# Sliding-window attention and a routed expert layer in one kernel: queries in one transfer, and the expert blocks begun in attention's last steps

## The chip, the cores and the metric

The kernel runs on one core of one Trainium2 chip. The metric is the device time of one execution in microseconds (us). Before the change three runs gave 413.17, 415.88 and 416.45 us; their median is 415.88. PE is TensorE (PEld its weight loads), DVE is VectorE, ACT is ScalarE, POOL is GpSimd, SP is SyncE, which here only issues transfers.

## The reference

```
# attention: B=8 batches, H=8 heads, S=576 positions, D=64
scores = (q @ k.T) / sqrt(D) - slope[h] * |i - j|,  kept where 0 <= i - j < 128
x = softmax(scores) @ v                        # as 4608 tokens x 512

# layer on x: w1_dense, w2_dense, and E=8 experts of 512 x 512 twice
y_dense = relu(x @ w1_dense) @ w2_dense
e = argmax(x @ w_gate);  g = softmax(x @ w_gate)[e]
out = y_dense + g * (relu(x @ w1[e]) @ w2[e])
```

Inputs and outputs are float32.

## The kernel before

**Attention.** A unit `u` is four heads of one batch: 16 units, two to a batch. A unit has three steps (query tiles 0-1, 2-3, and the tail 4), so there are `NS` = 48 steps. In step `n` the program emits, in this order: `flip` of step n-3 (PE transposes the normalized output, ACT copies it twice, L531), `scores` of step n (mask L405 and q times k L417 on PE, exp on ACT L428), `norm` of step n-2 (DVE L496, L497; POOL copies the rows, L503), parts of routing, `attend` of step n-1 (PE L481), parts of the dense layer (`dense1` L689/L696, `dense2` L704/L712), the preparation of the next unit, and `lo` of step n (DVE L447, the low halves of the weights). PE, ACT and DVE run this order as written (`manual_schedule`); POOL's order is set by the framework.

**Queries and keys.** A unit's `kraw` and `qraw` have one buffer each. k comes in one transfer: 18 rows of the sequence to a partition, 4608 contiguous bytes. q comes in five transfers (L140): 4 rows to a partition four times, then 2 rows. In step 0 of a unit DVE transposes the next unit's k (`turn`, L162), in step 1 its q; ACT rounds k in step 1 (L172) and q in step 2 (L169). The rounding of k puts the positions back in order by a strided write; q stays permuted within a tile, and the mask and the token numbers are built to that order. v comes in five transfers (L154) of 256-byte rows into three buffers. All loads after the first are issued on SP's queue, in program order.

**Routing and experts.** After a batch's two units its gate is computed (`gate_a` to `gate_d`), its 576 rows are scattered to their experts' regions in HBM (`xs_dram`, POOL L643), and its dense outputs to `ys_dram` (POOL L713). Then `NB` = 43 blocks of 128 rows follow: `fetch` (SP L901 loads a block's rows xr and yr), `turn_x` (PE L916, DVE L922), `layer1` (PE L937, ACT L945), `turn_h` (PE L952, ACT L956), `layer2` (PE L964, DVE L972, and POOL L973 scatters to the output). The first `NE` = 16 blocks hold rows of the first six batches, and their table (`route_early`) is computed while the last units run. The other 27 need all batches, the late table, and eight pairs of fill transfers (`late_fill`, SP L878 and L882) that pad the experts' last blocks. Blocks begin at loop step n = 50, two steps after the last `attend`; the dense work of batches 6 and 7 lies between the first blocks.

## Time and profile before

| | us |
|---|---|
| profiled execution | 411.29 |
| its span | 409.6 |
| median of three runs | 415.88 |
| PE / DVE / ACT / POOL busy | 339.0 / 269.8 / 261.6 / 192.9 |

The span is what the trace covers; 1.7 us of the profiled execution lie around it. Attention fills about the first 274 us, the blocks the rest up to 400 us. Busy shares are means over these two parts, so the rows below are taken from stretches.

### The profile page before, as it was taken

What the parts mean: (1) busy time and instruction counts of PE and PEld (TensorE: products, weight loads), DVE (VectorE), ACT (ScalarE), POOL (GpSimd) and SP (SyncE); (2) the same over time, 40 slices, a digit from 0 to 9 for tenths busy, and PEclk for the clock granted to TensorE, in tenths of its full rate; (3) what the DMA queues carried; (4) which work ended last, traced back from release to release, by engine and by line L of the source; (5) the groups of instructions that cost most, each with busy time, mean ns of one, the idle gap of its engine ahead of it and who ended that gap; (6) DMA issues with size and microseconds to landing.
All of it is one profiled execution on the core that took longest, in us unless ns stands there. A gap on an engine that the chain in (4) does not pass through costs nothing.

```text
span 409.6 us, 12253 instructions
## 1 busy us (share of the span) xinstructions
PE 339.0 (83%) x4659; PEld 215.2 (53%) x4659; DVE 269.8 (66%) x525; ACT 261.6 (64%) x431; POOL 192.9 (47%) x245
## 2 busy tenths in 40 slices
PE   3458887979869998968997996978799799999990
PEld 0245666646555665645664764654455455555540
DVE  6668889787867986957897889752346344444440
ACT  6448847857856986984797786644356445555550
POOL 4012331654765447564566576353457434434431
PEclk9999959989978999997999998999999999999996
DMA  4565678859798779788696965429959999888730
GB/s 146 144 159 142 148 172 193 195 173 238 165 235 180 202 204 218 212 188 225 197 226 195 235 179 116 99 70 338 310 172 323 303 311 324 244 264 234 250 117 1
DMA packets 84986, 82.40 MB, mean 201 GB/s; under 512 B 43583, under 2 KB 71615, under 8 KB 84928
## 3 DMA queue, kind: packets, MB, share of 16 engines
q1 hardware_dynamic: 66852, 48.17, 41.2%
q0 software_dynamic: 17680, 33.12, 31.3%
q8 instruction: 38, 0.62, 0.6%
q10 hardware_dynamic: 396, 0.33, 0.3%
q14 instruction: 20, 0.16, 0.1%
HBM read 64.20 MB, written 28.66 MB: 227 GB/s over the span
## 4 chain that ended last, share of the span: by engine, by line
PE 30%; DMA 19%; DVE 18%; issue 13%; POOL 9%; SPq 6%; ACT 2%; POOLq 1%; ACTq 0%; DVEq 0%
DMA qraw<-in_q_dram 16%; POOL out_dram L973 6%; DVE plo L447 6%; PE yp L704 6%; PE ax L481 6%; SPq L140 5%; DVE qs L162 4%; PE hpm L937 3%; PE y L964 3%; PE hp L689 3%; DVE xf L497 2%; PE lg L566 2%; DMA xr<-xs_dram 2%; DMA xs_dram<-xrow,slot 2%; PE sq L417 1%
## 5 line engine op out<-in xcount | busy, mean ns | idle before, releaser
L481 PE MATMUL ax<-vf,p 128*128 128x65 bf16 (+1 forms) x576 | 66.6, 205 | 28.8 <-DVE xf L497 26.4
L447 DVE TENSOR_TENSOR plo<-p 128x1024 bf16<-128x1024 f32 (+1 forms) x96 | 85.2, 928 | 8.0 <-ACT p L428 7.9
L481 PEld LDWEIGHTS <-p 128*128 128x128 bf16 (+1 forms) x1152 | 62.9, 107 | 41.3 <-DVE xf L497 34.9
L428 ACT ACTIVATE p<-sq 128x1024 f32<-128x1024 f32 (+1 forms) x96 | 69.8, 784 | 4.8 <-PE sq L417 4.6
L973 POOL DMA_INDIRECT out_dram<-yo,xr x43 | 42.4, 986 | 64.5 <-DVE yo L972 54.1
L503 POOL CAST xrow<-xf 128x512 bf16<-128x512 f32 (+1 forms) x48 | 33.2, 700 | 71.5 <-DVE xf L497 66.7
L481 PE MATMUL ax<-vf,plo 128*128 128x65 bf16 (+1 forms) x576 | 66.1, 202 | 0.5 <-DVE plo L447 0.5
L481 PE MATMUL ax<-vl,p 128*128 128x64 bf16 (+1 forms) x576 | 66.2, 201 | 0.0
L481 PEld LDWEIGHTS <-plo 128*128 128x128 bf16 (+1 forms) x576 | 58.7, 106 | 0.7 <-DVE plo L447 0.7
L713 POOL DMA_INDIRECT ys_dram<-yt,slot x40 | 45.7, 1142 | 26.7 <-ACT yt L712 17.9
L643 POOL DMA_INDIRECT xs_dram<-xrow,slot x40 | 46.2, 1154 | 14.6 <-issue 10.2
L922 DVE COPY xTm<-xps 128x512 bf16<-128x512 bf16 x43 | 18.3, 424 | 50.1 <-PE xps L916 46.9
L696 ACT ACTIVATE hTd<-hp 128x256 bf16<-128x256 f32 (+1 forms) x64 | 26.4, 419 | 35.5 <-PE hp L689 34.6
L937 PE MATMUL hpm<-w_all,xTm 128*128 x172 | 44.0, 377 | 5.1 <-DVE yo L972 2.1
L704 PE MATMUL yp<-w_all,hTd 128*128 128x512 bf16 (+1 forms) x160 | 40.6, 381 | 6.7 <-DVE ltsb L559 5.0
L964 PE MATMUL y<-w_all,hTm 128*128 x172 | 44.1, 379 | 0.8 <-ACT hTm L956 0.8
L945 ACT ACTIVATE hr<-hpm,xr 128x512 bf16<-128x512 f32 x43 | 29.6, 687 | 22.5 <-PE hpm L937 19.3
L972 DVE TENSOR_TENSOR yo<-y,yr 128x512 f32<-128x512 f32 x43 | 29.7, 691 | 20.7 <-PE y L964 20.1
L689 PE MATMUL hp<-xTb,w_all 128*128 128x256 bf16 (+1 forms) x256 | 42.4, 296 | 0.6 <-ACT xTb L531 0.3
L956 ACT COPY hTm<-hps 128x512 bf16<-128x512 bf16 x43 | 25.2, 585 | 23.2 <-PE hps L952 23.2
L531 ACT COPY xT<-tp 128x512 f32<-128x512 f32 (+1 forms) x48 | 23.9, 498 | 23.3 <-PE tp L524 23.2
L417 PE MATMUL sq<-qT,kT 32*128 32x256 f32 (+2 forms) x640 | 32.0, 310 | 7.0 <-ACT qT L169 7.0
(146 smaller groups left out, 559.7 us busy)
## 6 DMA issues: line engine op xcount, KB each, us to landing
yr<-ys_dram SPq DMA_DIRECT2D x43, 256.0 KB
kraw<-in_k_dram SPq DMA_DIRECT2D x16, 576.0 KB
vf<-in_v_dram SPq DMA_DIRECT2D x64, 128.0 KB
w_all<-in_moe_w_dram POOLq DMA_DIRECT2D x16, 512.0 KB
qraw<-in_q_dram SPq DMA_DIRECT2D x62, 128.0 KB
xr<-xs_dram SPq DMA_DIRECT2D x43, 130.0 KB
ys_dram<-fill_x SPq DMA_DIRECT2D x8, 256.0 KB
xs_dram<-fill_x SPq DMA_DIRECT2D x8, 130.0 KB
```

What stands on the lines that cost most here:

```text
L417: nc.tensor.matmul(out=sq[g // 2][:, g % 2, i * wid : i * wid + nq], lhsT=kT[32 * g : 32 * g + 32, c, kj * P : kj * P + P], rhs=qT[32 * g ...
L428: nc.scalar.activation(out=p32[:, :, 0:tot], in_=sq[i][:, :, 0:tot], func=ACT.Exp, scale=SCALE,)
L447: nc.vector.tensor_tensor(out=plo[:, :, 0:tot], in0=p32[:, :, 0:tot], in1=phi[:, :, 0:tot], op=ALU.subtract,)
L481: nc.tensor.matmul(out=ax[:rows, i, o0 : o0 + w], lhsT=lhs, rhs=rhs, start=(n == 1), stop=(n == 3 * len(kl)),)
L503: nc.gpsimd.tensor_copy(out=xrow[:rows, qis[0] : qis[0] + nt, hq * 256 : hq * 256 + 256], in_=xf[:rows, 0:nt],)
L643: ins = nc.gpsimd.indirect_dma_start(out=xs_dram[:, :], out_offset=bass.IndirectOffsetOnAxis(ap=slot[:rows, t : t + 1], axis=0), in_=xrow. ...
L689: nc.tensor.matmul(out=hp[:, 0:HF], lhsT=w_all[:, E, 0, kc, c * P : c * P + P], rhs=xTb[:, kc, c0:c1], start=(kc == 0), stop=(kc == 3),)
L704: nc.tensor.matmul(out=yp[:rows, :], lhsT=hT[:, c, t0 * P : t0 * P + rows], rhs=w_all[:, E, 1, c, :], start=(c == 0), stop=(c == 3),)
L713: ins = nc.gpsimd.indirect_dma_start(out=ys_dram[:, :], out_offset=bass.IndirectOffsetOnAxis(ap=slots[b][:rows, t : t + 1], axis=0), in_=y ...
L937: nc.tensor.matmul(out=hp, lhsT=xT[:, kc, :], rhs=w_all[:, bass.DynSlice(er, 1), 0, kc, :], start=(kc == 0), stop=(kc == 3),)
L964: nc.tensor.matmul(out=y, lhsT=hT[:, c, :], rhs=w_all[:, bass.DynSlice(er, 1), 1, c, :], start=(c == 0), stop=(c == 3),)
L973: ins = nc.gpsimd.indirect_dma_start(out=out[:, :], out_offset=bass.IndirectOffsetOnAxis(ap=xr.bitcast(I32)[:, TC : TC + 1], axis=0), in_= ...
```

## The change

Each unit's q comes in one transfer of the same form as k's, and its rounding takes the same strided write as k's; mask, token numbers and their helpers lose the permutation. The first unit's q is issued on ACT's queue, its rounding is done by DVE, the second unit's q is issued on ACT's queue too, the POOL copy that held back a part of the first v is gone, and `more_constants` moves on DVE from ahead of the first q to the end of step 1. SP runs in program order throughout. The pools of raw and transposed q and k stand on the other side of the memory, and are closed at step `NS` - 3; there five of now twelve block buffers are opened and the first five blocks fetched. The early table is computed in three steps in place of five. The first blocks begin right after the last `attend`, and what is left of batches 6 and 7 is put at fixed places in blocks 0 to 8 (`first`, `fill`).

```diff
--- before.py
+++ after.py
@@ pools
-    ld = ph1.enter_context(tc.tile_pool(name="ld", bufs=1))
-    stg = ph1.enter_context(tc.tile_pool(name="stg", bufs=1))
+    raws = ctx.enter_context(ExitStack())
+    ld = raws.enter_context(tc.tile_pool(name="ld", bufs=1, side="right"))
+    stg = raws.enter_context(tc.tile_pool(name="stg", bufs=1, side="right"))
@@ loads of k and q
+    def load_qk(u, nm, eng):
+        b, hq = divmod(u, HQ)
+        t = ld.tile([P, R, 2, 32], F32, name=f"{nm}raw", tag=f"{nm}raw")
+        eng.dma_start(
+            out=t.rearrange("p r c d -> p (r c d)"),
+            in_={"q": q, "k": k}[nm][b, 4 * hq : 4 * hq + 4].rearrange(
+                "h (p r) d -> (h p) (r d)", r=R
+            ),
+        )
+        raw[(nm, u)] = t
...
     def load_q(u, eng):
-        t = ld.tile([P, R, 2, 32], F32, name="qraw", tag="qraw", bufs=1)
-        for i in range(NT):
-            n = 4 if i < NT - 1 else 2
-            (eng[i] if isinstance(eng, tuple) else eng).dma_start(
...
+        load_qk(u, "q", eng)
@@ rounding of q and k
-    def round_qk(u, nm):
+    def round_qk(u, nm, copy=nc.scalar.copy):
         s = tmp.pop((nm, u))
         if nm == "q":
             d = qtp.tile([P, 2, S], F32R, name="qT", tag="qT", bufs=1)
-            nc.scalar.copy(out=d, in_=s)
         else:
             d = kTs[u % 2]
-            nc.scalar.copy(
-                out=d[:, :, 0:S].rearrange("p c (x r) -> p c r x", r=R),
-                in_=s.rearrange("p c (r x) -> p c r x", r=R),
-            )
+        copy(
+            out=d[:, :, 0:S].rearrange("p c (x r) -> p c r x", r=R),
+            in_=s.rearrange("p c (r x) -> p c r x", r=R),
+        )
@@ first loads
+    ctx.enter_context(tc.manual_schedule(engines={ENG.SP}))
     load_k(0)
-    load_q(0, (nc.scalar, nc.sync, nc.scalar, nc.sync, nc.scalar))
+    load_q(0, nc.scalar)
...
-    nc.gpsimd.tensor_copy(out=vfs[0][:, 0, 0, 0:1], in_=raw[("q", 0)][:, R - 1, 1, 31:32])
     load_v(0)
     wg_load()
@@ more_constants: the four m_div/m_mod/m_divf/m_modf operations and five scalar_tensor_tensor go
         for i in range(NT):
...
             nc.vector.tensor_scalar_add(
-                out=tok_c[:, i : i + 1], in0=tok_c[:, i : i + 1], scalar1=float(i * P)
+                out=tok_c[:, i : i + 1], in0=pidx_f, scalar1=float(i * P)
             )
@@ dense2
-        yt = xpool.tile([P, DM], F32, name="yt", tag="yt", bufs=4)
+        if b < B - 1:
+            yt = xpool.tile([P, DM], F32, name="yt", tag="yt", bufs=4)
+        else:
+            yt = mpool.tile([P, DM], F32, name="ytz", tag="ytz", bufs=NT)
@@ fetch
-        xr = mpool.tile([P, RW], F32, name="xr", tag="xr", bufs=10)
-        yr = mpool.tile([P, DM], F32, name="yr", tag="yr", bufs=10)
+        pool, n = (apool, NA) if j % NR < NA else (mpool, NR - NA)
+        xr = pool.tile([P, RW], F32, name="xr", tag="xr", bufs=n)
+        yr = pool.tile([P, DM], F32, name="yr", tag="yr", bufs=n)
@@ block
-    AHEAD = 7
+    NA, NR = 5, 12
+    nxt = [NR]
     def block(j):
-        if j == 0:
-            turn_x(0)
-            layer1(0)
-            turn_x(1)
+        for f in first.get(j, ()):
+            f()
+        mid = list(fill.get(j, ()))
         turn_h(j)
+        if mid:
+            mid.pop(0)()
         if j + 1 < NB:
             layer1(j + 1)
         if j + 2 < NB:
             turn_x(j + 2)
         layer2(j)
-        if j + AHEAD + 1 < NB:
-            fetch(j + AHEAD + 1)
+        for f in mid:
+            f()
+        ready = NB if j >= 8 else NE
+        while nxt[0] < min(j + NR + 1, ready):
+            fetch(nxt[0])
+            nxt[0] += 1
@@ main loop
         round_qk(0, "k")
-        more_constants()
-        mask_rest()
         turn(0, "q")
-        round_qk(0, "q")
+        round_qk(0, "q", nc.vector.tensor_copy)
+        mask_rest()
         load_k(1)
-        load_q(1, nc.sync)
+        load_q(1, nc.scalar)
+        load_v(1)
...
-        while jm < NB:
-            if n == NS:
-                loads.close()
-            if n > NS + 1:
-                block(jm)
-                jm += 1
+        for n in range(NS + 1):
...
-                            gates.setdefault(n + 4 + i, []).append(
+                            gates.setdefault(n + 4 + i // 2, []).append(
                                 lambda g=gen: next(g, None)
                             )
-                        gates.setdefault(n + 9, []).append(early_used)
+                        gates.setdefault(n + 7, []).append(early_used)
...
-            if n == 0:
-                load_v(1)
+            if n == 1:
+                more_constants()
...
+            if n == NS - 3:
+                raws.close()
+                apool = ctx.enter_context(
+                    tc.tile_pool(name="apool", bufs=1, side="right", reuse_waits="tile")
+                )
+                for j in range(NA):
+                    fetch(j)
...
+        first = {
+            1: [lambda: gate_av(last_u)],
+            2: [lambda: gate_bv(z)],
+            3: [lambda: gate_cv(z), lambda: gate_d(z)],
+            4: [late_counts, part],
+            5: [part, late_fill],
+            6: [part],
+            7: [part],
+        }
+        fill = {
+            0: [lambda: flip(*steps[NS - 1]), rest[0], lambda: gate_a(last_u)],
+            1: [rest[1], rest[2], lambda: gate_b(z)],
+            2: [rest[3], rest[4], lambda: gate_c(z)],
+            3: [rest[5], rest[6]],
+        }
+        for i, f in enumerate(dz):
+            fill.setdefault(4 + i // 3, []).append(f)
+        turn_x(0)
+        flip(*steps[NS - 2])
+        layer1(0)
+        turn_x(1)
+        for j in range(NA, NR):
+            fetch(j)
+        for j in range(NB):
+            block(j)
```

Three places where the order of instructions moves. First SP's queue, the loads of one unit in mid-attention (kraw, qraw and vf are the buffers of k, q and v), before and then in the change:

```order
L128 DMA kraw<-in_k_dram 128x1152
L140 DMA qraw<-in_q_dram 128x1x256 x4
L140 DMA qraw<-in_q_dram 128x1x128
L154 DMA vf_137<-in_v_dram 128x4x64 x4
L154 DMA vf_137<-in_v_dram 64x4x64
```

```order
L129 DMA kraw<-in_k_dram 128x1152
L129 DMA qraw<-in_q_dram 128x1152
L149 DMA vf_130<-in_v_dram 128x4x64 x4
L149 DMA vf_130<-in_v_dram 64x4x64
L129 DMA kraw<-in_k_dram 128x1152
```

The sequence k, q, v stays; five issues of q are one. Second, SP's queue at the end of the fills (sta and stb are the early and the late table of block starts, base_r the ends of the experts' regions), before and then in the change:

```order
L871 TENSOR_LOAD base_r
L878 ISA
L878 DMA xs_dram<-fill_x 128x260
L882 ISA
L882 DMA ys_dram<-fill_x 256x1x256
L891 TENSOR_LOAD sta
L901 ISA
L901 DMA xr<-xs_dram 128x260
```

```order
L840 TENSOR_LOAD base_r
L847 ISA
L847 DMA xs_dram<-fill_x 128x260
L851 ISA
L851 DMA ys_dram<-fill_x 256x1x256
L860 TENSOR_LOAD stb
L871 ISA
L871 DMA xr<-xs_dram 128x260
```

Before, the last two early blocks (14 and 15) are fetched behind the fills; in the change all 16 are fetched ahead of them. Third, PE between the last `attend` and the first `layer1` (yp and hp are dense products, tp the flip, xps and hpm those of a block), before and then in the change:

```order
L704 MATMUL yp<-w_all,hTd 128x512
L524 MATMUL tp<-ident_f,xf 128x128 x4
L689 LDWEIGHTS w_all
L689 MATMUL hp<-xTb,w_all 128x320
...
L916 MATMUL xps<-ident_129,xr 128x128
L937 LDWEIGHTS xTm
L926 TENSOR_LOAD era
```

```order
L670 MATMUL yp<-w_all,hTd 128x512
L886 LDWEIGHTS xr
L886 MATMUL xps<-ident_127,xr 128x128
...
L490 MATMUL tp<-ident_f,xf 128x128 x4
L907 LDWEIGHTS xTm
L896 TENSOR_LOAD era
```

The first block's transposes now follow the last dense product at once, and the eight hp products that stood ahead of them lie in blocks 0 and 1.

## Rows read from the trace of the kernel before

**Rows 1.** The page: the span, and the chain that ended last by line.

```profile
span 409.6 us, 12253 instructions
DMA qraw<-in_q_dram 16%; POOL out_dram L973 6%; DVE plo L447 6%; PE yp L704 6%; PE ax L481 6%; SPq L140 5%; DVE qs L162 4%; PE hpm L937 3%; PE y L964 3%; PE hp L689 3%; DVE xf L497 2%; PE lg L566 2%; DMA xr<-xs_dram 2%; DMA xs_dram<-xrow,slot 2%; PE sq L417 1%
```

**Rows 2.** Waits, whole span: engine, line, waited for: us in total, times, longest.

```profile
DVE qs L162 <- DMA qraw<-in_q_dram: 11.7, 6, 4.1
...
PE sq L417 <- ACT qT L169: 7.0, 1, 7.0
```

**Rows 3.** Timeline of DVE, transposes of q: start us, us, what, idle before.

```profile
65.92 1.38 DVE L162 STREAM_TRANSPOSE qs<-qraw 128x1152 f32<-128x1152 f32 x1
...
98.92 1.38 DVE L162 STREAM_TRANSPOSE qs<-qraw 128x1152 f32<-128x1152 f32 x1 [0.46 <-DMA qraw<-in_q_dram]
...
132.94 1.38 DVE L162 STREAM_TRANSPOSE qs<-qraw 128x1152 f32<-128x1152 f32 x1
...
163.41 1.38 DVE L162 STREAM_TRANSPOSE qs<-qraw 128x1152 f32<-128x1152 f32 x1
...
180.88 1.38 DVE L162 STREAM_TRANSPOSE qs<-qraw 128x1152 f32<-128x1152 f32 x1 [4.08 <-DMA qraw<-in_q_dram]
...
198.24 1.38 DVE L162 STREAM_TRANSPOSE qs<-qraw 128x1152 f32<-128x1152 f32 x1
...
211.55 1.36 DVE L162 STREAM_TRANSPOSE qs<-qraw 128x1152 f32<-128x1152 f32 x1
...
228.56 1.38 DVE L162 STREAM_TRANSPOSE qs<-qraw 128x1152 f32<-128x1152 f32 x1
```

**Rows 4.** Timeline of SP's queue: issue of one q and of the next k.

```profile
164.82 6.64 SPq L140 DMA_DIRECT2D qraw<-in_q_dram  x5
...
180.25 0.54 SPq L128 DMA_DIRECT2D kraw<-in_k_dram  x1
```

**Rows 5.** Chain of waits in order of time, its longest piece: start us, us, what.

```profile
85.67 13.22 DMA qraw<-in_q_dram
```

**Rows 6.** Groups by line, ACT's two roundings: busy us, mean ns | idle before.

```profile
L172 ACT CAST kT<-ks 128x1152 fp32r<-128x1152 f32 x16 | 37.5, 2345 | 0.0
...
L169 ACT CAST qT<-qs 128x1152 fp32r<-128x1152 f32 x16 | 18.4, 1147 | 3.5 <-DVE qs L162 3.5
```

**Rows 7.** Timeline of batch 6's first unit, from 205 to 222 us.

```profile
205.57 1.15 ACT L169 CAST qT<-qs 128x1152 fp32r<-128x1152 f32 x1
...
206.81 0.75 PE L417 MATMUL sq<-qT,kT 32*128 32x256 f32 x16
...
208.66 2.36 DVE L447 TENSOR_TENSOR plo<-p 128x1024 bf16<-128x1024 f32 x2 [0.40 <-ACT p L428]
...
217.52 0.37 POOL L636 TENSOR_SCALAR xrow<-tok_c 128x5 int32<-128x5 f32 x1 [4.97 <-DMA xs_dram<-xrow,slot]
...
221.18 0.69 DVE L497 TENSOR_TENSOR xf<-ax,recip 128x512 f32<-128x512 f32 x1 [2.86 <-POOL w_all L732]
```

**Rows 8.** Windows: stretch: us, busy of PE, PEld, DVE, ACT, POOL, clock, DMA, GB/s.

```profile
180.90:198.20 17.30, 12.73 (x174) 8.21 (x178) 13.27 (x21) 8.73 (x17) 10.02 (x11) 0.80 0.89 211
198.20:213.00 14.80, 13.89 (x286) 9.93 (x279) 13.92 (x25) 13.47 (x24) 8.50 (x10) 1.00 0.81 204
276.40:334.00 57.60, 50.35 (x349) 27.56 (x348) 23.38 (x68) 28.48 (x53) 28.11 (x31) 1.00 0.87 289
334.00:400.00 66.00, 64.52 (x441) 34.57 (x439) 30.85 (x55) 35.58 (x56) 27.73 (x29) 1.00 0.77 243
```

**Rows 9.** Timeline of the start, DVE's first transpose of k.

```profile
4.69 1.38 DVE L162 STREAM_TRANSPOSE ks<-kraw 128x1152 f32<-128x1152 f32 x1 [0.77 <-DMA kraw<-in_k_dram]
```

**Rows 10.** Timeline of PE, last flip but one, and the first block's first layer.

```profile
274.10 0.60 PE L524 MATMUL tp<-ident_f,xf 128*128 128x128 f32 x4
...
278.07 1.02 PE L937 MATMUL hpm<-w_all,xTm 128*128 x4 [1.23 <-POOL xrow L503]
```

**Rows 11.** One line, L878: duration ns min/median/max, first and last start us.

```profile
L878 SPq DMA_DIRECT2D xs_dram<-fill_x x8: 347/348/368, 304.8 to 321.1; - x8
```

More of the change, by code (lines that the diff above doesn't have):

```diff
@@ L112 @@
     )
-    kTs, vfs, xrows = [], [], []
+    kTs, xrows = [], []
     NV = 3
@@ L123 @@
     vparts = {}
[L125 to L146 removed]
+    def load_qk(u, nm, eng):
[8 more added lines that the diff above has]
+        raw[(nm, u)] = t
+    def load_k(u):
+        load_qk(u, "k", nc.sync)
+    def load_q(u, eng):
+        load_qk(u, "q", eng)
     def load_v(u):
@@ L199 @@
     sh = sh.rearrange("p c x -> p (c x)").bitcast(F32)
-    nc.gpsimd.iota(
-        d_i[:, 0:PW], pattern=[[P, 2], [1, 4], [4, 32]], base=0, channel_multiplier=-1
-    )
-    nc.gpsimd.iota(
-        d_i[:, PW : PW + P], pattern=[[1, 4], [4, 32]], base=0, channel_multiplier=-1
-    )
-    nc.gpsimd.iota(
-        d_i[:, PW + P : PW + P + TAIL],
-        pattern=[[1, 2], [2, 32]],
-        base=P,
-        channel_multiplier=-1,
-    )
-    nc.gpsimd.iota(
-        d_i[:, PW + P + TAIL : 2 * PW],
-        pattern=[[1, 2], [2, 32]],
-        base=0,
-        channel_multiplier=-1,
-    )
+    for c0, w, base in (
+        (0, PW, 0),
+        (PW, P, 0),
+        (PW + P, TAIL, P),
+        (PW + P + TAIL, TAIL, 0),
+    ):
+        nc.gpsimd.iota(
+            d_i[:, c0 : c0 + w], pattern=[[1, w]], base=base, channel_multiplier=-1
+        )
     pidx_i = consts.tile([P, 1], I32, name="pidx_i")
@@ L229 @@
     )
-    for i in range(NV):
-        vf = abuf.tile([P, NT, 4, D + 1], F32, name=f"vf{i}")
-        nc.gpsimd.memset(vf[TAIL:P, NT - 1, :, :], 0.0)
-        nc.gpsimd.memset(vf[:, :, :, D : D + 1], 1.0)
-        vfs.append(vf)
+    last = (NU - 1) % NV
+    order = [i for i in range(NV) if i != last]
+    vfs = {i: abuf.tile([P, NT, 4, D + 1], F32, name=f"vf{i}") for i in order}
     for i in range(2):
@@ L239 @@
         kTs.append(kT)
+    vfs[last] = abuf.tile([P, NT, 4, D + 1], F32, name=f"vf{last}")
+    for i in range(NV):
+        nc.gpsimd.memset(vfs[i][TAIL:P, NT - 1, :, :], 0.0)
+        nc.gpsimd.memset(vfs[i][:, :, :, D : D + 1], 1.0)
     for i in range(2):
@@ L1119 @@
                     fetch(j)
-            n += 1
         assert wnext == 2 * (E + 1)
+        norms.pop(NS - 1)()
+        ph1.close()
+        mpool = ctx.enter_context(
+            tc.tile_pool(name="mpool", bufs=3, reuse_waits="tile")
+        )
+        psum_t, psum_h, psum_y = [
+            ctx.enter_context(
+                tc.tile_pool(
+                    name=nm, bufs=2, space=bass.MemoryType.PSUM, reuse_waits="tile"
+                )
+            )
+            for nm in ("psum_t", "psum_h", "psum_y")
+        ]
@@ new lines @@
+        z, y = B - 1, B - 2
+        rest = [f for i in range(3) for f in items.pop(NS + 1 + i, [])]
+        dz = [f for fs in dense_items(z) for f in fs]
+        last_u = NU - 1
+        gen = late_table()
+        part = lambda: next(gen, None)
+        first = {
[7 more added lines that the diff above has]
+        }
@@ new lines @@
+        fill = {
[4 more added lines that the diff above has]
+        }
+        assert len(rest) == 7 and not items and set(gates) <= {NS + 1}
+        for i, f in enumerate(dz):
[4 more added lines that the diff above has]
+        turn_x(1)
```

64 lines of the change are left out of this document (1 added, 63 removed).

## The prediction

> **What bounds the kernel now.** I read the page first, then the waits, the transposes of q on DVE's timeline, SP's queue, and windows. On the page the reader is to see that the costliest line of the chain is no engine's work: 16% of the span is the landing of q, and 5% more its issue [rows 1]. That is a share of a chain, not a gain. The waits give a better size: DVE, which takes q out of its one buffer, sat idle for it 11.7 us in six waits [rows 2]. DVE's timeline shows what such a wait costs. From a batch's first q to the next batch's first q pass 33.0 us (65.92 to 98.92), 34.0, 30.5 (132.94 to 163.41), 34.8 and 30.3 (198.24 to 228.56) [rows 3]. The two short ones hold no wait for q; the longest holds the longest wait, 4.08 us. So about 30.4 us is the batch's period when q is in time, and what sets it then must be found inside it, since the change also lengthens an ACT instruction there.
>
> In batch 6 the half from 198.20 to 213.00 keeps PE busy for 13.89 of 14.80 us, DVE for 13.92 and ACT for 13.47 [rows 8]: nothing is spare. In the other half DVE stands 2.86 us ahead of a normalization, released by POOL, and POOL stood 4.97 us for the landing of its own scatter [rows 7]. That scatter is started by the gate, ahead of anything that ACT's rounding of q delays. So a clean batch has 2.86 us of slack at that point.
>
> After 276 us the blocks run: PE is busy 50.35 of 57.60 us to 334, and 64.52 of 66.00 after it [rows 8]. The 27 late blocks are PE's; only the first part has idle time to win.
>
> **The change part by part.** The sum is made against the profiled execution, 411.3 us with a span of 409.6. The median of the three runs stands 4.6 us above it; all three lie higher.
>
> *q in one transfer.* SP spends 6.64 us issuing the five parts of one q, and 0.54 us on the one transfer of k [rows 4]. The last part of a q then took up to 13.22 us to land [rows 5]. With one issue the whole q is out some 6.1 us earlier. Take the worst case of the rows: issue at 164.8, 0.5 us of issue and the longest landing give 178.6, and DVE came to it at 176.8 (180.88 less 4.08) [rows 3]. Even so 1.8 of 4.08 us would be left, with the 10 us or so usual for the others nothing. I take all waits as gone. In batches 2 to 6 that makes five periods of 30.4, 152.0, from 162.6 us (65.92 to 228.56): a gain of 10.6. Ahead of 65.92 there is one more wait among the six; I put it and its echo on PE at 1.5 us (ends 0.5 and 3).
>
> *q rounded by a strided write.* ACT's rounding of q is 1.15 us; the same amount written in k's pattern is 2.35 [rows 6]. So each of 15 units adds 1.20 us on ACT, 2.4 to a batch. It lies on the path: PE's product with q starts at 206.81, 0.09 after the rounding ends, and DVE's subtraction after it waited 0.40 for ACT [rows 7]. In the full half nothing hides it. Where both halves' 2.4 us arrive at the normalization, POOL's 2.86 us of slack take them; behind that point the second 1.2 us still delay scores and exp, and I leave 0.7 us to a batch. Five batches lose 3.6 us, so the 10.6 become **7.0**. The ends: no loss, and with lighter queues a scatter that lands 0.3 us sooner per batch (12), or all of 2.4 us uncovered (12.0 against 10.6, a loss of 1.4). If POOL's wait went, the cover would be gone and the period would be near 30.4 - 2.9 + 2.4 = 29.9, no worse.
>
> *The start.* PE's first product with q waited 7.0 us for the rounded q [rows 2]. k, the same size in one transfer, was there at 4.69 [rows 9]; two of them side by side I put at 6 to 8. Then DVE transposes (1.38 [rows 3]) and rounds q, at 1.15 to 2.35 us: no row has a strided copy on DVE, so ACT's two rows bound it, and I take the upper. The exp of step 0 then waits for the masks on ACT, and comes some 3 us sooner than before. The Trainium skill, "SBUF — State Buffer", section "Door 1: The DMA port swizzle (why `[64,N]` ≈ `[32,N]`)", says that accesses within one 16-byte line go at full rate and each crossing to a new line pays; by it the upper value holds, and by the lower one the sum would gain 1.2 us. Most of the 3 us is given back: the second k and q have to come too, on SP's queue behind five issues of v and on ACT's behind the masks, and `more_constants` now stands between step 1 and the first normalization, with 2 to 3 us of DVE. I take **2.0** gained (ends 5 gained, 1.5 lost).
>
> *The last units.* There is no scatter wait to hide ACT's 2 x 1.2 us after 228.56, one wait for q of about 1 us goes, and the early table's small DVE work is pressed into three busier steps. I take **1.5 lost** (ends 1 gained, 4 lost).
>
> *The blocks.* Between the flip at 274.10 and the first layer of block 0 at 278.07 [rows 10] stand two dense products, the fetch's landing and two waits. In the change five blocks have been fetched three steps earlier, and xps, flip and the first layer follow each other: 274.1 + 0.4 + 0.6 gives 275.1, 3.0 us sooner, but 1.7 us of dense products come later instead, and 1.3 stay. Then the idle time: 7.25 us of PE from 276.4 to 334, 1.5 after. Before, the fills hold SP's queue from 304.8 to past 321 [rows 11], ahead of blocks 14 and 15; now these are fetched first. What stays idle is the wait for the first blocks' own chain and the loading of expert numbers. I take 3.2 of 7.25 as won, together **4.5** (ends 8 gained, 3 lost).
>
> Each move has its queue. The first five fetches stand on SP behind the last v and ahead of nothing but more fetches, so their wait for the dense rows of batch 5 holds nobody up. The second q's issue stands on ACT behind the masks and ahead of the first exp, and can wait there for a v to land: that is inside the ends of the start. On POOL the attention part keeps its order.
>
> The sum: 2.0 + 1.5 + 7.0 - 1.5 + 4.5 = 13.5 us. From 411.3 that is 397.8, from the median 402.4. A median is forecast, but the runs shown spread by 3.3 us and the profiled one lies below them, so I take the middle, **400 us**.
>
> **The rivals.**
>
> *ACT takes it back.* For it: ACT 13.47 of 14.80 us in the full half [rows 8], and a rounding that PE and DVE wait for to within 0.1 and 0.4 us. Against it: the 2.86 us on POOL. If nothing is hidden, the batches lose 1.4 in place of gaining 7.0, and the last units one more: 13.5 - 9.4 = 4.1 gained, 407 from the profiled time, 409.5 on the footing of the forecast. Chance 0.16.
>
> *The transfer is no faster, and half the waits stay.* For it: DMA's share is 0.81 to 0.89 in those stretches [rows 8], v's ten-odd us of small rows stay, and q may stand behind them however it is cut. The Trainium skill, "DMA: Bandwidth & Descriptors", section "Specifications", gives 512 bytes as the least transfer for line rate; q's old rows had 1024 and 512 bytes, so by it larger rows buy nothing. Against it: the issue time alone is 6.1 us per unit. Half of 11.7 us kept makes 5.9 less: about 406. Chance 0.05.
>
> *Slower: the clock falls.* In the half behind the 4.08 us wait PE ran with a mean granted clock of 0.80, partly at the lower of its two levels (1.2 and 2.4 GHz), in the clean half at 1.00 [rows 8]. If ACT's longer rounding made PE stand in every unit as long as DVE stood in that wait, one half of each batch would run so, and PE's 12.73 us there hold 2.5 us that full clock would save; with seven batches 17.5 us on top of the first rival's 409.5 is 427. It decides from a wait of PE of some 4 us a unit; 1.2 us does not reach that, and the waits that did are those that go. Chance 0.06.
>
> *The blocks begin no earlier*, since a fetch waits for rows of batch 5 or late blocks stand behind fills: the 4.5 go to 0, about 404.5. That lies in the forecast's own range.
>
> **How the numbers follow.** The forecast has 0.70, the rivals 0.16, 0.05 and 0.06, and 0.03 is left for what I don't see. The forecast's own range is 391 to 407: start, batches and blocks at their better ends together would give 20 us, at half their worse ends 6. The range for 8 in 10 reaches up over most of the first rival, and a little down for lighter queues: 389 to 411. About 1% (4.2 us) is what a measurement of this kernel can tell from no change. Faster by more, below 411.7: the forecast nearly whole, the second rival and most of the first, 0.82. Within 1%: the rest of the first and a forecast that misses twice, 0.11. Slower: 0.07.
>
> **What would show it.** In the new profile the landing of q should be gone from the chain's lines, DVE's waits for it be near 0, and SP's issue of q near 0.5 us. ACT's rounding of q should read 2.35 us and add 18 us to ACT. Batches should follow each other every 31 us; 33 would speak for ACT, with PE's product standing behind the rounding. The first exp should come 3 us sooner, the first layer of block 0 right behind the flip, and PE's idle time up to the late blocks halve. I would be wrong above all if POOL's wait for its scatter grew or went together with DVE's load, or if the dense work put between blocks 0 and 8 starved the blocks.

## The result and the profile after

The changed kernel takes **391.81 us** (median of four runs, 390.85 to 393.85) beside 415.06 us (413.17 to 416.45) for the kernel before on the same chip: a ratio of 0.945, 95% interval 0.939 to 0.951. Forecast were 400 us and a range of 389 to 411. Its profiled execution took 391.61 us, with a span of 389.9; that of before 411.3 and 409.6. All sizes below are differences of these two traces, 19.7 us in all. From here on a median or a ratio leaves out the runs that lie over 1.5% above the fastest of their kernel on the same chip.

The page answers [rows 1]. No landing and no issue of q is left in the chain; DVE's `plo`, PE's products and ACT's rounding of q have taken their place.

```profile
span 389.9 us, 12097 instructions
...
PE 45%; DVE 23%; ACT 13%; issue 8%; POOL 3%; DMA 3%; SPq 1%; POOLq 0%; DVEq 0%; ACTq 0%
DVE plo L413 11%; PE ax L447 10%; PE yp L670 8%; PE hpm L907 8%; ACT qT L166 7%; PE y L934 7%; PE hp L655 3%; DVE xf L463 3%; DVE qs L157 3%; ACT p L394 3%; DMA kraw<-in_k_dram 2%; PE sq L383 2%; POOL out_dram L943 2%; PE lg L532 2%; PE xps L886 2%
```

The waits over the whole span answer [rows 2] (engine, line, waited for: us in total, times, longest). DVE's wait for q is gone from the list. PE's wait for the rounded q has become many short ones where it was one of 7.0 us.

```profile
PE sq L383 <- ACT qT L166: 12.8, 12, 1.1
...
POOL xrow L602 <- DMA xs_dram<-xrow,slot: 9.1, 6, 2.3
...
DVE ks L157 <- DMA kraw<-in_k_dram: 3.3, 2, 3.2
```

DVE's timeline (start us, us, what, idle before) from the start, and its transposes of q that answer [rows 3]:

```profile
6.62 1.38 DVE L157 STREAM_TRANSPOSE ks<-kraw 128x1152 f32<-128x1152 f32 x1 [3.17 <-DMA kraw<-in_k_dram]
7.92 1.34 DVE L157 STREAM_TRANSPOSE qs<-qraw 128x1152 f32<-128x1152 f32 x1
9.29 1.24 DVE L166 CAST qT<-qs 128x1152 fp32r<-128x1152 f32 x1
...
21.82 0.20 DVE L462 RECIPROCAL recip<-ax 128x8 f32<-128x8 f32 x1
...
32.30 1.36 DVE L157 STREAM_TRANSPOSE qs<-qraw 128x1152 f32<-128x1152 f32 x1
...
59.10 1.37 DVE L157 STREAM_TRANSPOSE qs<-qraw 128x1152 f32<-128x1152 f32 x1
...
90.09 1.37 DVE L157 STREAM_TRANSPOSE qs<-qraw 128x1152 f32<-128x1152 f32 x1
...
214.12 1.37 DVE L157 STREAM_TRANSPOSE qs<-qraw 128x1152 f32<-128x1152 f32 x1
...
231.16 1.36 DVE L157 STREAM_TRANSPOSE qs<-qraw 128x1152 f32<-128x1152 f32 x1
```

From 59.10 to 214.12 are five batches, so 31.0 us to a batch; the halves are 14.4 and 16.6 us in every one. Before, the periods ran from 30.3 to 34.8.

SP's queue, one q, answers [rows 4]; the groups by line (busy us, mean ns | idle before) answer [rows 6]:

```profile
215.52 0.34 SPq L129 DMA_DIRECT2D qraw<-in_q_dram  x1
```

```profile
L166 ACT CAST kT<-ks 128x1152 fp32r<-128x1152 f32 x16 | 37.5, 2345 | 1.9 <-DVE ks L157 1.9
L166 ACT CAST qT<-qs 128x1152 fp32r<-128x1152 f32 x15 | 35.2, 2348 | 0.0
```

The timeline of batch 6's first unit answers [rows 7]. POOL's wait for its scatter is 2.32 us where it was 4.97, and DVE's wait for POOL 0.87 where it was 2.86.

```profile
199.81 0.47 POOL L602 TENSOR_SCALAR xrow<-tok_c 128x5 int32<-128x5 f32 x1 [2.32 <-DMA xs_dram<-xrow,slot]
...
205.08 0.69 DVE L463 TENSOR_TENSOR xf<-ax,recip 128x512 f32<-128x512 f32 x1 [0.87 <-POOL w_all L701]
```

Windows (stretch: us, busy of PE, PEld, DVE, ACT, POOL, clock, DMA, GB/s) answer [rows 8]: both halves of batch 6, then the early and the late blocks.

```profile
183.11:197.55 14.44, 12.47 (x256) 8.75 (x252) 12.48 (x23) 13.21 (x23) 8.58 (x10) 1.00 0.91 224
197.55:214.12 16.57, 14.76 (x255) 9.77 (x252) 12.67 (x23) 13.90 (x22) 10.66 (x13) 1.00 0.88 198
259.79:317.39 57.60, 53.58 (x373) 30.51 (x379) 25.41 (x71) 31.80 (x59) 31.15 (x33) 1.00 0.81 279
320.00:380.00 60.00, 57.72 (x391) 31.39 (x397) 28.09 (x50) 32.42 (x51) 24.91 (x26) 1.00 0.74 240
```

The clock is full in both halves. Counted as before from the first block's transposes, PE's idle time in 57.6 us of blocks is 4.0 us, where it was 7.25.

PE's timeline at the first block answers [rows 10], and the line of the fills (duration, first and last start) answers [rows 11]; blocks 14 and 15 are now fetched at 278.8 and 288.6, ahead of them.

```profile
259.79 0.39 PE L886 MATMUL xps<-ident,xr 128*128 128x128 bf16 x4
260.02 0.61 PE L490 MATMUL tp<-ident_f,xf 128*128 128x128 f32 x4
261.44 1.02 PE L907 MATMUL hpm<-w_all,xTm 128*128 x4 [0.81 <-POOL xrow L469]
```

```profile
L847 SPq DMA_DIRECT2D xs_dram<-fill_x x8: 350/351/378, 290.2 to 305.6; - x8
```

### The profile page after: what moved, and what is told of

Same layout as the page of the kernel before. It is cut to its first block, busy times and chain, and to the rows that moved or that the text cites. A ratio compares the mean times of both kernels' runs of the same rounds, so it can differ in the third digit from the quotient of the medians.

```text
span 389.9 us, 12097 instructions
## 1 busy us (share of the span) xinstructions
PE 329.4 (84%) x4631; PEld 210.1 (54%) x4659; DVE 266.8 (68%) x517; ACT 276.2 (71%) x430; POOL 196.1 (50%) x244
## 4 chain that ended last, share of the span: by engine, by line
PE 45%; DVE 23%; ACT 13%; issue 8%; POOL 3%; DMA 3%; SPq 1%; POOLq 0%; DVEq 0%; ACTq 0%
DVE plo L413 11%; PE ax L447 10%; PE yp L670 8%; PE hpm L907 8%; ACT qT L166 7%; PE y L934 7%; PE hp L655 3%; DVE xf L463 3%; DVE qs L157 3%; ACT p L394 3%; DMA kraw<-in_k_dram 2%; PE sq L383 2%; POOL out_dram L943 2%; PE lg L532 2%; PE xps L886 2%
## 5 line engine op out<-in xcount | busy, mean ns | idle before, releaser
L447 PE MATMUL ax<-vf,p 128*128 128x65 bf16 (+1 forms) x576 | 63.3, 201 | 16.4 <-DVE xf L463 16.4
L447 PEld LDWEIGHTS <-p 128*128 128x128 bf16 (+1 forms) x1152 | 59.8, 104 | 28.9 <-DVE xf L463 22.6
L447 PE MATMUL ax<-vl,p 128*128 128x64 bf16 (+1 forms) x576 | 62.8, 197 | 0.0
L447 PE MATMUL ax<-vf,plo 128*128 128x65 bf16 (+1 forms) x576 | 62.6, 198 | 0.0
L682 POOL DMA_INDIRECT ys_dram<-yt,slot x35 | 46.9, 1340 | 28.4 <-ACT yt L681 21.7
L469 POOL CAST xrow<-xf 128x512 bf16<-128x512 f32 (+1 forms) x48 | 30.7, 647 | 54.2 <-DVE xf L463 51.7
L447 PEld LDWEIGHTS <-plo 128*128 128x128 bf16 (+1 forms) x576 | 56.8, 103 | 0.0
L907 PE MATMUL hpm<-w_all,xTm 128*128 x162 | 42.3, 377 | 4.4 <-issue 1.7
L662 ACT ACTIVATE hTd<-hp 128x256 bf16<-128x256 f32 (+1 forms) x64 | 26.4, 419 | 20.8 <-PE hp L655 20.3
L655 PE MATMUL hp<-xTb,w_all 128*128 128x256 bf16 (+1 forms) x256 | 41.1, 289 | 0.0
L166 ACT CAST kT<-ks 128x1152 fp32r<-128x1152 f32 x16 | 37.5, 2345 | 1.9 <-DVE ks L157 1.9
```

What stands on the lines that cost most here:

```text
L166: copy(out=d[:, :, 0:S].rearrange("p c (x r) -> p c r x", r=R), in_=s.rearrange("p c (r x) -> p c r x", r=R),)
L447: nc.tensor.matmul(out=ax[:rows, i, o0 : o0 + w], lhsT=lhs, rhs=rhs, start=(n == 1), stop=(n == 3 * len(kl)),)
L655: nc.tensor.matmul(out=hp[:, 0:HF], lhsT=w_all[:, E, 0, kc, c * P : c * P + P], rhs=xTb[:, kc, c0:c1], start=(kc == 0), stop=(kc == 3),)
L682: ins = nc.gpsimd.indirect_dma_start(out=ys_dram[:, :], out_offset=bass.IndirectOffsetOnAxis(ap=slots[b][:rows, t : t + 1], axis=0), in_=y ...
L907: nc.tensor.matmul(out=hp, lhsT=xT[:, kc, :], rhs=w_all[:, bass.DynSlice(er, 1), 0, kc, :], start=(kc == 0), stop=(kc == 3),)
```

## The experiments

They ran on four other chips, and each is compared with runs of before on its own chip. On all four, before takes 438 to 441 us, not 415; on the two where the changed kernel ran it takes some 2% less, not 5.5%. So first what differs there: the trace of the kernel with one pool (below; its attention is the changed kernel's). Windows, the two halves of a batch, there:

```profile
126.32:144.77 18.45, 13.27 (x243) 8.74 (x236) 12.59 (x24) 13.02 (x22) 9.41 (x12) 0.93 0.72 181
144.77:163.68 18.91, 17.05 (x275) 11.52 (x264) 13.02 (x23) 14.26 (x23) 8.65 (x10) 0.89 0.69 165
```

and the same batch of the changed kernel on the chip of the result:

```profile
121.09:135.54 14.45, 12.48 (x255) 8.76 (x252) 12.47 (x23) 13.20 (x23) 8.58 (x10) 1.00 0.88 221
135.54:152.09 16.55, 14.73 (x255) 9.74 (x252) 12.66 (x22) 13.88 (x22) 9.82 (x11) 1.00 0.77 200
```

DVE and ACT are busy for the same time within 0.5 us, yet the batch takes 37.4 us, not 31.0. PE is busy for 30.3 us, not 27.2, at a mean granted clock of 0.93 and 0.89 in place of 1.00; whether the lower clock comes of the longer batch or the other way round isn't shown. Waits of that trace name no engine and no transfer of the kernel ("issue": nothing that the profile shows; "remote": a signal that it can't place):

```profile
DVE xTm L892 <- remote: 7.6, 1, 7.6
...
PE ax L447 <- issue: 6.1, 9, 1.2
...
PE hpm L907 <- issue: 5.6, 6, 3.4
...
PE yp L670 <- issue: 4.0, 4, 3.1
ACT xT L497 <- remote: 4.0, 1, 4.0
...
ACT p L394 <- remote: 3.6, 1, 3.6
```

On the chip of the result the changed kernel has no "remote" wait, and PE's two rows of "issue" there are 1.7 and 1.0 us. That the kernel before has such stalls on those chips is inferred from its times; no trace of it was taken there. What causes them stays open. What the runs can tell in spite of them: differences of whole kernels on one chip, and the first 57 us, in which no wait is "remote" and PE's waits on "issue" sum to 1.2 us at most.

The traces can also be cut at the transposes of q, as in the account below (us; the first two rows are the chip of the result, the others are the runs that follow):

| kernel | to the fifth q | five batches, to the fifteenth | to the sixteenth | from there to the end |
|---|---|---|---|---|
| before | 65.9 | 162.6 | 15.1 | 165.9 |
| changed | 59.1 | 155.0 | 17.0 | 158.7 |
| q alone (second run) | 56.8 | 176.0 | 16.7 | 185.6 |
| q in five | 69.6 | 178.9 | 20.4 | 174.6 |
| old order of the start | 59.0 | 177.2 | 19.4 | 179.7 |
| one pool | 56.9 | 177.2 | 19.4 | 175.7 |
| q rounded contiguously | 58.7 | 175.8 | 19.0 | 178.1 |
| order restored by the transpose | 64.9 | 182.3 | 20.0 | 180.6 |
| q on DVE | 60.6 | 168.3 | 20.8 | 180.1 |
| q on DVE, k read with stride (two runs) | 60.5, 59.8 | 164.1, 161.0 | 20.8, 20.8 | 178.2, 176.6 |

**q alone** (twice), on the kernel before:

```
-        for i in range(NT):
...
+        eng.dma_start(
+            out=t.rearrange("p r c d -> p (r c d)"),
+            in_=q[b, 4 * hq : 4 * hq + 4].rearrange("h (p r) d -> (h p) (r d)", r=R),
+        )
...
-            nc.scalar.copy(out=d, in_=s)
+        nc.scalar.copy(
+            out=d[:, :, 0:S].rearrange("p c (x r) -> p c r x", r=R),
+            in_=s.rearrange("p c (r x) -> p c r x", r=R),
+        )
```

> The kernel before with one edit: q comes in one transfer, and ACT restores its order with a strided write (2.35 us in place of 1.15). Start order and tail are those of before. My theory: the five batches go to a period of 31 us each (from 32.5 on average), some 7 us, the wait ahead of 65.92 gives 1.5 to 2, the last units take 1 back, the start gives under 1.5 because the constants still stand ahead of q: 8 to 9 us less than before, about 403 beside the 411.3 of the profiled run, ratio 0.98. Rival 'all from q': start and tail bring nothing of their own, then this kernel is at the changed kernel's time, ratio 0.945. Rival 'ACT takes it back': ratio 0.99 or more, with batches at 32.5.

> The kernel before with only q in one transfer, as in the first run, once more. If before takes 415 here and the stalls without a releaser are absent: theory 'start from q, attention from q, tail from order' reads the changed kernel's trace as 5 us at the first normalization, 1.75 up to 65.92 and 7.6 in five batches, all q's, and about 4 at the first block and 3 in the blocks, the tail's; then q alone gives 13 to 15 us less a loss of 1 in the last units, ratio 0.967 to 0.972. Rival 'all of it is q': 0.945. Rival 'the new order of the start counts': 0.98. If before takes 440 or more: ratio 0.975 to 0.98, as the changed kernel itself there.

**q in five transfers again**, with the mask and the token numbers that go with its old order; the rest of the change is kept:

```
+        for i in range(NT):
...
+            copy(out=d, in_=s)
...
-    load_q(0, nc.scalar)
+    load_q(0, (nc.scalar, nc.sync, nc.scalar, nc.sync, nc.scalar))
...
-        load_q(1, nc.scalar)
+        load_q(1, nc.sync)
```

> The changed kernel with q in five transfers again, its order left as it arrives and rounded by a contiguous copy; the new start order (with the five issues of the first q on two queues as before), the early fetches and the new tail stay. My theory: it loses the 7.6 us of the five batches and about 2 ahead of them, and wins back about 1 to 2 in the last units where ACT's 1.2 us go: 8 to 9 us above the changed kernel, ratio to before 0.965. Rival 'all from q': it is back at the time of before, ratio 1.0. Rival 'the start sets it': under 4 us above the changed kernel, ratio 0.955.

**The changed kernel, as control** (twice):

> The changed kernel itself, once more, as the control for the other runs of this call and, if before again takes some 447 us, of the four runs before. Where before takes 415: ratio 0.945. Where it takes 447, by the stalls without a visible releaser that the traces of that chip show on TensorE, ACT and DVE: theory 'the gain stands, the stalls come on top' says 447 less 20 to 24, ratio 0.95; rival 'the stalls eat it' says 0.97 to 0.98, beside the 0.978 of the kernel with one pool.

> The changed kernel as the control of the next run, on one chip with it. Ratio to before 0.945 where the stalls without a releaser are absent, 0.975 to 0.98 where they are there.

Measured: q alone 430.0 (a single run) where before took 440.0, and 433.0 beside 441.0, ratio 0.981 (0.975 to 0.987). q in five 442.6, ratio 1.004 (0.986 to 1.022). The changed kernel 432.1 where before took 441.4, ratio 0.978 (0.968 to 0.988), and 430.8 beside 437.9, ratio 0.986 (0.980 to 0.992). So on these chips q's transfer brings what can be measured in whole times, and without it the rest shows no gain: 'all from q' holds for q in five, and the figures that I gave for either side of the split (0.965 for q in five) fall. The changed kernel gains 7 to 9 us there and not 23, as the control's rival said; that it is the stalls that take the rest isn't shown.

The stretches tell where. What q in five loses lies ahead of its fifth q: 69.6 us (before, on the chip of the result, 65.9), where the kernels with one transfer and DVE's transpose unchanged have 56.8 to 60.6. Its five batches take 178.9 us, beside 175.8 to 177.2 with q in one transfer, that transpose and the rounding on ACT. So the 7.6 us that the five batches gave on the chip of the result are not repeated here by an experiment.

The starts can be read. DVE's timeline of the kernel with q alone, at the first normalization and the third q:

```profile
23.20 0.20 DVE L459 RECIPROCAL recip<-ax 128x8 f32<-128x8 f32 x1
...
31.41 1.36 DVE L157 STREAM_TRANSPOSE qs<-qraw 128x1152 f32<-128x1152 f32 x1
```

and of the kernel with q in five transfers and the new order:

```profile
12.02 1.38 DVE L168 STREAM_TRANSPOSE qs<-qraw 128x1152 f32<-128x1152 f32 x1 [5.89 <-DMA qraw<-in_q_dram]
...
24.16 1.38 DVE L168 STREAM_TRANSPOSE qs<-qraw 128x1152 f32<-128x1152 f32 x1 [3.90 <-DMA qraw<-in_q_dram]
...
31.65 0.20 DVE L505 RECIPROCAL recip<-ax 128x8 f32<-128x8 f32 x1
```

Before, the first normalization stood at 26.95 and the third q at 37.37; in the changed kernel at 21.82 and 32.30. The transfer alone brings 3.75 and 5.96 us of it; the second run of q alone has both marks within 0.05 us of the first. The order without the transfer makes the normalization 4.7 us later than before. With the transfer it wins 1.4 us at the first normalization and has lost 0.9 by the third q. That second figure is within what kernels of the same start differ by: the one with one pool, on the same chip as this q alone, has 22.03 and 31.50, so that the order wins 1.2 us and by the third q nothing: given back.

**The old order of the start**, in the changed kernel:

```
-        turn(0, "q")
-        round_qk(0, "q", nc.vector.tensor_copy)
+        more_constants()
         mask_rest()
+        turn(0, "q")
+        round_qk(0, "q")
...
-            if n == 1:
-                more_constants()
```

> The changed kernel with the work of the first steps in its old order: the block of constants and the second half of the masks ahead of q's transpose, and q's first rounding on ACT. Transfers, attention and tail stay new. My theory after reading the new profile: the first normalization comes 5.1 us earlier in the changed kernel, and most of it is this order; it comes back here, 4 to 5 us above the changed kernel, ratio 0.955 to 0.957 to before. Rival 'given back' (what the prediction thought): the second k and q are what step 3 waits for whatever the order, so it is 1 to 2 us above, ratio 0.948 to 0.95. A third: the single transfer alone brings the start forward and the order nothing, ratio 0.945.

Measured: 436.25 beside 440.0 for before on the same chip; ratio 0.989 (0.982 to 0.995). Its first normalization comes at 22.93, 1.1 us behind the changed kernel's, and its third q at 32.70, 0.4 behind; beside the kernel with one pool, on the same chip, it is 0.9 and 1.2 behind. So my re-reading of the new profile, that the order was worth 4 to 5 us, was wrong by the start itself; 'given back', 1 to 2 us, is nearest. The whole times of these two kernels do differ by 5.2 us, but 4.0 of the 6.0 us between their traces lie behind the last q, where the start no longer works.

**One pool**: the first blocks' buffers from the pool that opens when attention's closes:

```
-        pool, n = (apool, NA) if j % NR < NA else (mpool, NR - NA)
+        pool, n = mpool, NR
...
-                for j in range(NA):
-                    fetch(j)
...
+        for j in range(NR):
+            fetch(j)
         turn_x(0)
```

> The changed kernel with the buffers of the first five expert blocks taken from the pool that opens when attention's is closed, as before; so their fetches wait for that memory. The order on PE, ACT and DVE stays new. My theory: the order of work alone starts the first block earlier, and the early fetch is worth only the time from the memory's release to the landing, 2 to 4 us: ratio 0.950 to 0.955. Rival 'order alone': 0 to 1 us, ratio 0.945 to 0.947. Rival 'fetch is all of it': 7 us, ratio 0.962.

Measured: 431.0, ratio 0.978 (0.968 to 0.987), as the control elsewhere. The edit did only half of what I meant. Its first fetch is issued 6.84 us behind the last q's transpose (260.41 after 253.57), in the changed kernel's control 6.82 (267.96 after 261.14): SP came to it no later. The fetches behind it do wait. SP issues the second block's yr there at the first of these lines, 1.0 us ahead of the first block's transposes (289.51), and in the changed kernel on the chip of the result at the second, 6.8 us ahead of them:

```profile
288.55 0.33 SPq L871 DMA_DIRECT2D yr<-ys_dram  x1
...
252.99 0.33 SPq L871 DMA_DIRECT2D yr<-ys_dram  x1
```

No loss shows for that: its last stretch, 175.7 us, is among the shortest. What a later first fetch would cost stays untried.

**What ACT's strided write costs**: q rounded by a contiguous copy, k and the rest as changed.

```
             d = qtp.tile([P, 2, S], F32R, name="qT", tag="qT", bufs=1)
+            copy(out=d, in_=s)
```

> The changed kernel with q rounded by a contiguous copy, so that the queries stay in the order in which the transpose leaves them: this leaves out the restoring of their order, and the output is that of permuted queries. It prices the strided write of ACT, 1.2 us in each unit. Theory 'ACT is on the path in every unit' (its rounding is a 2.35 us piece of the chain in each unit, and PE waits 12.8 us for it in 12 waits): a half batch gets 0.8 to 1.1 shorter, 10 to 13 us less than the changed kernel, period 29.2 to 29.5. The prediction's figure, 0.7 us left of it in a batch and more in the last units: 5 to 6 us less, period 30.3. Rival 'hidden': under 2 us.

Measured: 431.55 beside the control's 432.1, ratio to before 0.976 (0.967 to 0.985), the control's 0.978. ACT's rounding takes 1151 ns, and PE's wait for q is gone; ahead of that product it still waits for k, 3.6 us in the first unit. The difference of 0.6 us, with intervals of 2%, decides neither for the prediction's 5 to 6 us nor for 'hidden'. Its five batches take 1.5 us less than those of the last two kernels, at a granted clock of 0.91 beside their 0.95 and 0.96.

**The order restored by DVE's transpose**:

```
-        nc.vector.transpose(out=s.rearrange("p c (r x) -> p r c x", r=R), in_=t)
+        nc.vector.transpose(out=s.rearrange("p c (x r) -> p r c x", r=R), in_=t)
...
-            out=d[:, :, 0:S].rearrange("p c (x r) -> p c r x", r=R),
-            in_=s.rearrange("p c (r x) -> p c r x", r=R),
+        copy(out=d[:, :, 0:S], in_=s)
```

> The changed kernel with the order restored by DVE's transpose (its write goes to every 18th element), so that ACT rounds k and q by contiguous copies, 1.15 us each in place of 2.35. Theory: DVE rounds the first q with a strided write in 1.24 us, near what 1152 elements take it contiguously, so a strided write costs DVE nothing; the transposes stay at 1.37 us, ACT loses 2.4 us per unit, and the time is 10 to 16 us below the changed kernel. Rival: a strided write costs DVE what it costs ACT, the transposes go to 2.5 us each; then DVE has 2.3 us more per unit and, being 13.9 of 16.6 us busy in the full half, the time is 5 to 15 us above.

Measured: 447.0, ratio 1.009 (1.005 to 1.014), 14.9 us above the control, whose interval (0.968 to 0.988) ends below it. Its groups by line:

```profile
L157 DVE STREAM_TRANSPOSE ks<-kraw 128x1152 f32<-128x1152 f32 x16 | 37.3, 2330 | 3.2 <-DMA kraw<-in_k_dram 3.2
...
L166 ACT CAST kT<-ks 128x1152 fp32r<-128x1152 f32 x16 | 18.5, 1155 | 2.9 <-DVE ks L157 2.9
...
L166 DVE CAST qT<-qs 128x1152 fp32r<-128x1152 f32 x1 | 0.8, 759 | 0.0
```

The theory falls. The transposes went from 1.37 to 2.33 us, and DVE's contiguous rounding of q takes 0.76 us, not the 1.24 that I had taken for it. A strided write costs DVE too: 0.48 us on a copy, 0.96 on a transpose. What it adds to DVE counts for more than the 2.4 us per unit that ACT is spared.

**q rounded by DVE in every unit** (the first pair of lines), then also **k read with stride by ACT** (all lines; run twice, the second time beside the control):

```
-                        round_qk(u + 1, "q")
+                        round_qk(u + 1, "q", nc.vector.tensor_copy)
...
+        f = "p c r x" if nm == "q" else "p c x r"
...
-            out=d[:, :, 0:S].rearrange("p c (x r) -> p c r x", r=R),
-            in_=s.rearrange("p c (r x) -> p c r x", r=R),
+            out=d[:, :, 0:S].rearrange(f"p c (x r) -> {f}", r=R),
+            in_=s.rearrange(f"p c (r x) -> {f}", r=R),
```

> The changed kernel with q rounded by DVE in every unit (1.24 us there, as in the first unit) and not by ACT (2.35 us). Theory 'ACT's length sets it': PE's product with q comes up to 1.1 us sooner and DVE has 1.24 us more; the two balance to 2 to 6 us less than the changed kernel. Rival 'DVE is the bound of the half': 5 to 10 us more.

> The changed kernel with q rounded by DVE in every unit, and k rounded by ACT in the other loop order: it reads every 32nd element and writes one after the other. Theory 'the price of ACT is on its write': k's rounding falls from 2.35 to near 1.15 us, ACT loses 3.5 us per unit in all, and the time is 6 to 9 us below the changed kernel (0.925 to 0.93 where that has 0.945; 0.96 to 0.965 where it has 0.978). Rival 'a strided read costs the same': k stays at 2.3 us, and the time is that of the kernel with q on DVE alone, 4 to 7 us below the changed kernel.

> The changed kernel with q rounded by DVE in every unit and k rounded by ACT in the order of its reads, as in the run before. Theory 'ACT's rounding of q was still on the path': 5 to 9 us below the changed kernel on the same chip, a ratio of 0.98 to 0.988 to it. Rival 'the earlier difference was that of two chips': within 2 us of it.

Measured: q on DVE 429.75, ratio 0.973 (0.964 to 0.983), 2.4 below the control on its chip, which the intervals don't part. With k read with stride 426.0, ratio 0.968 (0.961 to 0.975), and 424.3, ratio 0.974 (0.968 to 0.980), beside the control's 430.8. On that chip the means of three runs and the control's five differ by 8.5 us, 95% interval 2.9 to 14.1: this kernel beats the changed one there, and before by 13.6 us. k's rounding by ACT in the other order still takes 2.23 us:

```profile
L167 ACT CAST kT<-ks 128x1152 fp32r<-128x1152 f32 x16 | 35.7, 2228 | 1.9 <-DVE ks L157 1.9
```

so the stride costs ACT nearly the same on the read side, and by these lengths the gain is mostly q's. In the kernel with q on DVE, PE waits for q once, in the first unit:

```profile
L383 PE MATMUL sq<-qT,kT 32*128 32x256 f32 (+2 forms) x640 | 32.8, 316 | 4.0 <-DVE qT L166 3.8 <-issue 0.2
...
L166 DVE CAST qT<-qs 128x1152 fp32r<-128x1152 f32 x16 | 19.9, 1242 | 0.1
```

What it takes on the chip of the result was not tried.

## Why the prediction was right, and where its terms were off

The time was in the range, near its lower end, and the faster side had 0.82. Of the 8.2 us below the forecast, 6.2 are the terms and 2.2 its footing (see the end of this section). By terms, in the two traces (the marks are the third, fifth, fifteenth and sixteenth transposes of q, and the end):

| term | forecast | measured |
|---|---|---|
| start, to the third q (37.37, now 32.30) | 2.0 | 5.1 |
| waits ahead of 65.92 (now 59.10) | 1.5 | 1.75 |
| five batches (162.64, now 155.02) | 7.0 | 7.6 |
| last units (15.11, now 17.04) | -1.5 | -1.9 |
| blocks, from the last q to the end (165.9, now 158.7) | 4.5 | 7.2 |
| sum | 13.5 | 19.7 |

*Waits for q and ACT's write.* In the two traces the mechanism held as written. All waits went, SP's issue is 0.34 us, ACT has 16.8 us more (18 forecast; the first unit's rounding went to DVE), and a batch takes 31.0 us (31 forecast): 0.6 above the clean 30.4, where 0.7 was left of ACT's 2.4. Two halves of before, one behind a wait for q and a clean one, show what the waits cost:

```profile
115.28:132.94 17.66, 14.19 (x202) 9.02 (x195) 14.11 (x21) 9.89 (x18) 10.20 (x12) 0.81 0.92 210
132.94:146.25 13.31, 12.39 (x256) 8.68 (x252) 12.48 (x23) 12.05 (x22) 7.49 (x9) 1.00 0.82 213
```

Of the ten halves in before's five batches, the three that begin behind a wait of DVE for q or v of 2.3 to 4.1 us have a clock of 0.80 to 0.90, the other seven 1.00; in the changed kernel all ten have 1.00. PE is busy for 29.0 to 29.3 us in those three batches, for 27.3 in each of the two clean ones and for 26.9 to 27.3 in those of the changed kernel. So of the 10.6 us that the three are longer than clean ones, 5.6 are PE's busy time at the lower clock. ACT's write shows where the forecast had it: the clean half of 13.31 us became 14.45, and PE waits up to 1.1 us a unit for q there; the other half, 17.16 when clean, is 16.55, since POOL's wait for its scatter shrank. The chain holds a 2.35 us piece of ACT in every unit of the five batches. That these gains are q's is read from the two traces; the experiments, on chips where the same attention takes 35 us and more to a batch, don't repeat them. Nor do they price ACT's write: q on DVE takes 9 to 16 us out of the five batches there, more than the whole term of 3.6, and the contiguous copy on ACT 1.5.

*The start* was mis-sized, at the step "most of the 3 us is given back". The first exp came 3.5 us sooner (12.14, before 15.60), as forecast. But I set the second k and q against it as a load that must come too, and not as one more q whose five issues go: it was at DVE at 23.41 after 3.06 us of wait, and now at 15.69 without one. (The profile of before names no releaser for that wait; with q in five the same one, 3.90 us, ends on q's landing.) The runs put nearly 6 us at the third q on the transfer and about nothing on the order. DVE's rounding took 1.24 us, near the lower bound; I took the upper. The Trainium skill, "SBUF — State Buffer", section "Door 1: The DMA port swizzle (why `[64,N]` ≈ `[32,N]`)", has each crossing to another 16-byte line pay. The rows agree that a strided write costs more, but not in one size: 0.48 us on DVE's copy, 0.96 on its transpose, 1.20 on ACT's.

*The last units* went as forecast in size: from 228.56 before and 214.12 after, the interval to the last q grew by 1.9 us. Of the reasons given, the moved work is the one that the runs point to and ACT's write is not: on the other chips the interval is 16.7 us in q alone, which has ACT's write and the old tail, and 19.0 to 20.8 in all kernels with the new tail, also where ACT's write of q is contiguous or gone.

*The blocks* gave 7.2 us, where 4.5 were forecast; two sizes in the term were too small. From the last q to the first block's transposes pass 28.63 us (32.78 before): the first block comes 4.15 us sooner, 3.0 forecast. PE's work in that interval fell from 26.94 to 23.88 us and its idle time from 5.84 to 4.75; 1.3 us of the work stand in the interval ahead (13.75, now 15.06). The rest comes later, as forecast (1.7): from those transposes to the last block's second layer PE now has the eight hp products and a flip, 1.9 us by their lines. PE's busy time there seems to deny it (114.81, now 113.89), but the trace of the changed kernel lacks records: of 172 products of each layer of the blocks, all there in that of before, it has 162 and 167.

```profile
L907 PE MATMUL hpm<-w_all,xTm 128*128 x162 | 42.3, 377 | 4.4 <-issue 1.7
L934 PE MATMUL y<-w_all,hTm 128*128 x167 | 43.4, 379 | 1.1 <-ACT hTm L926 0.8
...
264.43 0.81 PE L907 MATMUL hpm<-w_all,xTm 128*128 x3 [0.53 <-issue]
```

A group of four takes 1.02 us, this one with three records 0.81, and the missing 0.2 us reads as idle time; for 15 records that is some 3 us, an estimate. PE's idle time in this stretch reads 6.32 us (8.74 before); less those 3 us, with the stretch 3.3 us shorter (120.21, before 123.55) and 1.9 us more work in it, some 5 us of idle time went, where I had 3.2. On the other chips the last stretch of the table speaks for the new tail too: 185.6 us in q alone, which has the old one, and 174.6 to 180.6 in the eight others. That is one trace against eight, with stalls in just this stretch, so the size of the gain rests on the two traces of the chip of the result.

*The rivals.* 'ACT takes it back' would have shown periods of 33 us. 'Half of the waits stay' falls with the waits. That it was the issues and q's place in the queue that bounded it fits this, but no run has one issue with the old short rows, so issue and row size aren't parted. 'The clock falls' falls with a clock of 1.00 in both halves. Its condition, a wait of some 4 us, was set too high: behind DVE's waits of 2.3 and 3.0 us before had 0.90 and 0.81; PE's 1.1 us in the changed kernel left it at 1.00.

*Two readings in the prediction* were off without harm to its sum. The 6.64 us of issue are the longest of one q in before: the fifteen on SP's queue alone take 3.0 to 6.6, 4.7 on average, so 6.1 us per unit is an upper end. And the better ends of start, batches and blocks, with the other two terms as forecast, give 25 us (5 + 1.5 + 12 - 1.5 + 8), not 20, so that the forecast's own range should have begun lower.

The forecast of 400 also took the middle between the footing of the profiled run and that of the median. The median after lies at its profiled run, that of before 3.8 us above its own, so the medians differ by 23.3 us where the traces differ by 19.7.

## What to carry to other kernels

A load that is issued in pieces holds its queue for all of the issues (here 3.0 to 6.6 us for one q, 0.34 in one piece). Cutting it to one was worth the waits that it showed and the clock that fell behind them; for the start the experiments show that the transfer did it, for the batches only the two traces do. Price the layout work that this shifts to an engine by what that engine has beside it in the same unit, and then ask which other engine could do it: here the copy that ACT makes in 2.35 us takes DVE 1.24. A gain that is read as a difference of two traces belongs to no part of a change until a run with that part alone has shown it; my first reading gave the start to the order, and it was the transfer's. And count the records of both traces before comparing busy times: 15 lost products looked like 3 us of work that had gone.

## What the runs showed of the hardware that was not expected

The same program takes some 6% longer on four chips than on a fifth (438 to 441 us and 415), with instructions of DVE and ACT of the same length, a granted clock of 0.90 to 0.99 in the five batches (before on the fifth 0.95, the changed kernel 1.00), and stalls that no visible work releases, up to 8.6 us long. Of this change's gain of 23 us, 7 to 9 are left there. A price of stride is one of engine and instruction: 1152 floats a partition take DVE 0.76 us contiguous and 1.24 strided, ACT 1.15 contiguous, 2.35 with the stride on the write and 2.23 with it on the read.
